# A Strassen scheme for the up projection of four batches, and a joint read in the down projection

## The chip, the cores and the metric

The kernel runs on one core of a Trainium2 chip. A core has five engines that run side by side, each through its own list of instructions in order, held together by semaphores: TensorE (PE in the profile; matrix products, results in PSUM), VectorE (DVE), ScalarE (ACT), GpSimd (POOL; here only DMA issue) and SyncE (SP; DMA issue). PSUM has eight banks of 128 x 512 fp32; SBUF is the working memory.

The metric is the device time of one execution in microseconds (us). The kernel before takes 298.88 us, the median of 3 runs (298.83 to 299.14). The profiled execution spans 296.9 us from its first to its last instruction; profile times count from that start.

## What is computed

The program is a block-causal attention followed by an MLP mixer, for 8 batches, 576 positions, 8 heads of 64 (so 512 model columns). The reference, cut to what matters:

```python
# attention: q, k, v are (8, 8, 576, 64); blocks of 64 positions
scores = scale * q @ k.T                       # per batch and head
scores = where(block_i >= block_j, scores, -1e9)
attn = exp(scores - max) / (sum + 1e-9)
x = (attn @ v)                                 # as (8, 576, 512)

# mixer
h  = relu(x.T @ w_tok1) @ w_tok2               # over positions: 576 -> 256 -> 576
u  = x + h.T
h2 = relu(u @ w_ch1) @ w_ch2                   # over channels: 512 -> 1536 -> 512
out = u + h2                                   # float32
```

`u @ w_ch1` is called the up projection, `(...) @ w_ch2` the down projection. Matrix inputs are bf16, sums fp32.

## The kernel before

The kernel is written as a list of operations with dependencies, estimated costs and priorities. On the host a list scheduler (`Plan`) places them on the engines, tries 1000 random changes of the priorities, and issues the best order that it found. So a change of any operation can change the order of all.

Of each batch, 512 positions are treated on their own, and the last 64 of two batches together ("mixed" rows). The PSUM banks are split: four hold scores, as two pairs (`sc`), four are the general pool `mm`.

```python
sc = ring(2, [128, 2, 512], FP32, "sc", psum)     # 4 banks: scores
mm = ring(4, [128, 512], FP32, "mm", psum)        # 4 banks: all else
gT = ring(2, [128, NDC, 512], BF16, "gT")         # relu(u @ w_ch1), NDC = 12 blocks of 128 channels
sums = ring(3, [128, 3, NDC // 2, 128], BF16, "sums")
```

The up projection: for each of 12 blocks of hidden channels, four matmuls of 512 columns add up in a bank (L950), and ACT or DVE clips it at zero into `gT` (L725, L727).

```python
def channel_up(b, uT_done, wc1_ready, prio):
    for cc in range(NDC):
        def emit(o, ...):
            for m in range(NDM):                     # NDM = 4
                nc.tensor.matmul(out=bank_of(bank), lhsT=wc1_sb[:, m, channels(cc)],
                                 rhs=uT[b % 2][:, :, m, :], start=(m == 0), stop=(m == NDM - 1))   # L950
        op = P.add("PE", ..., take=[(BANK, bank)])
        def emit(o, ...):
            relu(o, gT[b % 2][:, cc, :], bank_of(bank))                        # L725 ACT, L727 DVE
        done.append(P.add(EVAC, evac_cost(512), emit, [op], prio, give=[bank]))
```

The down projection of batches 1 to 7 is already a Strassen scheme (the Winograd form): the product is cut into 2 x 2 blocks, and seven block products stand in for eight. The input sums are made on DVE from `gT` (L1032), products gather in banks (L1049), and DVE adds what a bank holds into the output tile after each product, so the bank goes on gathering (L1071). Rows 128 t and 128 t + 256 are one pair; t = 0, 1 are done one after the other.

```python
def channel_down_fast(b, g_done, wc2_ready, u_done, prio):
    for t in range(2):
        r1, r2 = slice(128 * t, 128 * t + 128), slice(128 * t + 256, 128 * t + 384)
        a11, a12 = gt[:, 0:H6, r1], gt[:, H6:NDC, r1]                      # H6 = 6
        a21, a22 = gt[:, 0:H6, r2], gt[:, H6:NDC, r2]
        for key, dst, x, y, op in (("s1", s1, a21, a22, ADD), ("s2", s2, s1, a11, SUB),
                                   ("s4", s4, a12, s2, SUB), ("s3", a21, a11, a21, SUB)):
            nc.vector.tensor_tensor(out=dst, in0=x, in1=y, op=op)          # L1032, 768 elements
        # product: six matmuls of 256 columns into one bank                  L1049
        # fold: o_sb[...] = bank[:, 0:256] + (u or o_sb)                     L1071
        fold("a", 0, 0, product(0, "a", a11, b11, []), True, False)
        fold("e", 1, 1, product(1, "e", s1, w1_, [made["s1"]]), True, False)
        ...                                                                # seven in all
```

Around it: token mixing makes `u` (matmuls L739 and L832, the addition of x on DVE at L847), a DMA transposes it into `uT` (a ring of two), and attention has scores (L511), exponentials on ACT (L530), the product with v (L558) and its scaling on DVE (L586). `L396` turns q and k from staging memory on DVE, `L1009` makes the sums of the down weights, `L356` copies a bank or a staged input.

Of the kernel before, what the change touches and what calls it, by code (L numbers as in the profile page):

```python
# [195 lines left out]
def kernel(  # L196
# [11 lines left out]
    nc = tc.nc  # L208
# [18 lines left out]
    qraw = ring(3, [128, NB, D], BF16, "qraw")  # L227
    kraw = ring(3, [128, NB, D], BF16, "kraw")

    qT = ring(3, [128, S, 2], BF16, "qT")  # L230
    kT = ring(3, [128, 640, 2], BF16, "kT")
    v1 = ring(2, [128, 5, H, 66], BF16, "v1")
    e_sb = ring(2, [128, 4, 1600], BF16, "e_sb")
    et_sb = ring(2, [128, 640], BF16, "et_sb")
# [8 lines left out]
    sums = ring(3, [128, 3, NDC // 2, 128], BF16, "sums")  # L243
    o_sb = ring(3, [128, 2, DM], FP32, "o_sb")
# [22 lines left out]
    BANK = ("mm",)  # L267
    WARM, KEEP = 16, 110

    def bank_of(note):  # L270
        return mm[note["slot"]]
# [256 lines left out]
    def exp(dst, n, op, note, prio, urgent=0):  # L528
        def emit(o):
            nc.scalar.activation(dst, sc[SC.index(note["pool"])][:, :, 0:n], EXP, scale=scale)  # L530

        return P.add("ACT", act_cost(2 * n), emit, [op], prio, give=[note], urgent=urgent)

    def mask(e, c, hs, deps, prio, urgent=0):
        def emit(o):
            nc.vector.memset(e[64:128, hs, c : c + 64], 0.0)  # L536

        return P.add("DVE", 0.1, emit, deps, prio, urgent=urgent)

    def head_out(b, head, deps, prio, tail, urgent=0):  # L540
# [41 lines left out]
        rc = P.add("DVE", 0.12, emit_rc, [av] + reuse(("rinv", head % 4)), prio - 1, urgent=urgent)  # L582
# [93 lines left out]
    def attention(b, ready, v_ready):  # L676
# [5 lines left out]
        def exps_of(op, notes, dst, n, prio):  # L682
            return [exp(dst[:, 2 * f : 2 * f + 2], n, op, notes[f], prio) for f in range(2)]
# [11 lines left out]
        tail_done = None  # L695
        for hg in range(2):
            e = e_sb[hg]
            prio = base + 4 * hg
            e_war = reuse(("e", hg))
            exps = [[], []]  # L700
            for s, regions in enumerate(SETS):
                n = sum(w for _, _, _, w in regions)
                parts = tuple((hg,) + r for r in regions)
                notes = [{}, {}]
                pools = [(SC[f : f + 1], notes[f]) for f in range(2)]
                op = score_set(b, parts, range(4), ready[hg] + e_war, prio + 0.1 * s, pools)
                these = exps_of(op, notes, e[:, :, 512 * s : 512 * s + n], n, prio + 0.1 * s)
                masks = [mask(e, c, slice(0, 4), these, prio) for c in MASKS[s]]
                for f in range(2):
                    exps[f] += [these[f]] + masks  # L710
            if tail_done is None:
                tail_done = tail()
            for h in range(4):
                deps = exps[h // 2] + v_ready[hg] + x_war + pad + pads["e", hg]
                done.append(head_out(b, 4 * hg + h, deps, prio + 1, tail_done[h // 2]))
# [89 lines left out]
    def token_mix(b, x_done, w1_ready, w2_ready):  # L805
        odd = b % 2
        pair = b // 2
        xt, at, ut, umt = x_sb[b % 3], aT[b % 2], u_sb[b % 3], um_sb[pair % 2]
        prio = -990.5 + 10 * b
        a_war = reuse(("a", b % 2))  # L810
        u_war = reuse(("u", b % 3))
# [77 lines left out]
        for f in range(2 if crossbar else 0):  # L889
# [7 lines left out]
            reads(("u", b % 3), op)  # L897
# [8 lines left out]
        for si in () if crossbar or b == 0 else range(4 + odd):  # L906
# [15 lines left out]
            reads(("u", b % 3) if si < 4 else ("um", pair % 2), op)  # L922
# [74 lines left out]

    H6 = NDC // 2
# [14 lines left out]
    def channel_down_fast(b, g_done, wc2_ready, u_done, prio):  # L1013
        gt, ut = gT[b % 2], u_sb[b % 3]
        for t in range(2):
            oi = out_n[0] % 3
            out_n[0] += 1
            o_war = reuse(("o", oi))
            si = sum_n[0] % 3
            sum_n[0] += 1  # L1020
            s_war = reuse(("s", si))
            r1, r2 = slice(128 * t, 128 * t + 128), slice(128 * t + 256, 128 * t + 384)
            a11, a12 = gt[:, 0:H6, r1], gt[:, H6:NDC, r1]
            a21, a22 = gt[:, 0:H6, r2], gt[:, H6:NDC, r2]
            s1, s2, s4 = (sums[si][:, n] for n in range(3))
            made = {}
            prev = None
            for key, dst, x, y, op in (
                ("s1", s1, a21, a22, ADD), ("s2", s2, s1, a11, SUB), ("s4", s4, a12, s2, SUB), ("s3", a21, a11, a21, SUB),
            ):  # L1030
                def emit(o, dst=dst, x=x, y=y, op=op):
                    nc.vector.tensor_tensor(out=dst, in0=x, in1=y, op=op)  # L1032

                prev = made[key] = P.add(
                    "DVE", dve_cost(768, 2), emit, (g_done + s_war if prev is None else [prev]), prio - 2 + 0.1 * t
                )
                reads(("g", b % 2), prev)
            b11, b21, b22 = wc2_sb[:, 0:H6, 0:256], wc2_sb[:, H6:NDC, 0:256], wc2_sb[:, H6:NDC, 256:512]
            w1_, w2_, w3_, w4_ = (wd_sb[:, n] for n in range(4))
            banks = {"a": {}, "c": {}, "e": {}}  # L1040
            last = {}
            stored = []

            def product(n, to, x, y, deps):
                bank, first = banks[to], to not in last

                def emit(o):
                    for kk in range(H6):
                        nc.tensor.matmul(  # L1049
                            out=bank_of(bank)[:, 0:256], lhsT=x[:, kk], rhs=y[:, kk],  # L1050
                            start=first and kk == 0, stop=kk == H6 - 1,
                            skip_group_check=not first,
                        )

                op = P.add(
                    "PE", mm_cost(256, H6), emit, deps + g_done + wc2_ready + wd_ready + [last.get(to)],
                    prio + 0.2 * t + 0.02 * n, take=[(BANK, bank)] if first else (),
                )
                reads(("g", b % 2), op)
                reads(("s", si), op)  # L1060
                last[to] = op
                return op

            def fold(to, row, col, op, residual, final):
                dst = o_sb[oi][:, row, 256 * col : 256 * col + 256]
                bank = banks[to]

                other = ut[:, t + 2 * row, 256 * col : 256 * col + 256] if residual else dst

                def emit(o):  # L1070
                    nc.vector.tensor_tensor(out=dst, in0=bank_of(bank)[:, 0:256], in1=other, op=ADD)  # L1071

                done = P.add(
                    "DVE", dve_cost(256), emit, [op, folded.get((row, col))] + u_done + o_war, prio - 1,
                    give=[bank] if final else (),
                )
                reads(("u", b % 3), done)
                folded[row, col] = last[to] = done
                return done

            folded = {}
            fold("a", 0, 0, product(0, "a", a11, b11, []), True, False)
            fold("e", 1, 1, product(1, "e", s1, w1_, [made["s1"]]), True, False)
            fold("a", 0, 1, product(2, "a", s2, w2_, [made["s2"]]), True, False)
            fold("e", 0, 1, product(3, "e", s4, b22, [made["s4"]]), False, True)
            fold("a", 1, 1, product(4, "a", a21, w3_, [made["s3"]]), False, False)
            fold("c", 0, 0, product(5, "c", a12, b21, []), False, True)
            fold("a", 1, 0, product(6, "a", a22, w4_, []), True, True)

            rows = out[b, 0:512, :].rearrange("(c t p) d -> t p c d", c=2, t=2)[t]  # L1090
            if b == B - 1 and t == 1:
                pieces = [(0, 0, 2), (1, 1, 2), (1, 0, 1)]
            else:
                pieces = [(None, 0, 2)]
            for row, c0, c1 in pieces:
                def emit(o, row=row, c0=c0, c1=c1, oi=oi, rows=rows):
                    cols = slice(256 * c0, 256 * c1)
                    if row is None:
                        nc.sync.dma_start(out=rows, in_=o_sb[oi])
                    else:  # L1100
                        nc.sync.dma_start(out=rows[:, row, cols], in_=o_sb[oi][:, row, cols])

                deps = [folded[r, c] for r in ((0, 1) if row is None else (row,)) for c in range(c0, c1)]
                size = (2 if row is None else 1) * (c1 - c0) / 2
                reads(("o", oi), P.add("SP", 0.5, emit, deps, prio, xfer=8 * 0.086 * size))
# [4 lines left out]
    def channel_down(b, g_done, wc2_ready, u_done, prio, mixed=False):  # L1110
        chunks = [None] if mixed else list(range(4))
        gt = gmT[0] if mixed else gT[b % 2]
        ut = um_sb[b // 2 % 2] if mixed else u_sb[b % 3]
# [3 lines left out]
        for n, si in enumerate(chunks):  # L1117
# [4 lines left out]
            if n % 2 == 0:  # L1122
                oi = out_n[0] % 3
# [3 lines left out]
            for cols in (slice(0, 256), slice(256, 512)) if last else (slice(0, 512),):  # L1127
# [32 lines left out]
                reads(("gm", 0) if mixed else ("g", b % 2), prev)  # L1160
# [15 lines left out]
                reads(("um", b // 2 % 2) if mixed else ("u", b % 3), op)  # L1176
# [36 lines left out]
    x_done = {}  # L1213
    for b in range(B + 1):
# [8 lines left out]
        if b > 0:  # L1223
            p = b - 1
            uT_done, um_done, u_done, um_rows = token_mix(p, x_done[p], w1_ready, w2_ready)
            g_done = channel_up(p, uT_done, wc1_ready, 10 * p + 2)
            if p == 0:
                channel_down(p, g_done, wc2_ready, u_done, 10 * p + 4)
            elif p < B - 1:
                channel_down_fast(p, g_done, wc2_ready, u_done, 10 * p + 4)  # L1230
            if p % 2 == 1:
                gm_done = channel_up_mixed(p // 2, um_done, wc1_ready, 10 * p + 3.5)
                prio = 10 * p + (5 if p < B - 1 else 3.9)
# [37 lines left out]
```

The softmax here doesn't subtract the row's maximum and nothing guards it: scores larger than these inputs give would overflow.

## Time and profile before

| | value |
|---|---|
| time, median of 3 | 298.88 us |
| span of the profiled execution | 296.9 us |
| TensorE matmuls busy | 290.8 us, 3257 instructions |
| VectorE busy | 203.7 us, 509 instructions |
| ScalarE busy | 164.4 us, 233 instructions |
| granted TensorE clock | 1.000 of full speed |
| up projection (L950) | 384 matmuls of 512 columns |
| clips of the up projection into `gT` | 76 on ACT, mean 597 ns; 20 on DVE, mean 688 ns |

The page gives for each engine its busy time, then the span in 40 equal slices in which a digit is the busy share in tenths, then the chain of work that ended last, by engine and by line, and then groups of instructions (line, engine, operation, out<-in, shape, number, busy us, mean ns). A table by stretches of time gives, for each stretch, its length and each engine's busy us with the number of instructions. Matmuls overlap one another in the pipeline, so the mean of one is longer than the time that it adds to a row of them.

### The profile page before, as it was taken

What the parts mean: (1) busy time and instruction counts of PE and PEld (TensorE: products, weight loads), DVE (VectorE), ACT (ScalarE), POOL (GpSimd) and SP (SyncE); (2) the same over time, 40 slices, a digit from 0 to 9 for tenths busy, and PEclk for the clock granted to TensorE, in tenths of its full rate; (3) what the DMA queues carried; (4) which work ended last, traced back from release to release, by engine and by line L of the source; (5) the groups of instructions that cost most, each with busy time, mean ns of one, the idle gap of its engine ahead of it and who ended that gap; (6) DMA issues with size and microseconds to landing.
All of it is one profiled execution on the core that took longest, in us unless ns stands there. A gap on an engine that the chain in (4) does not pass through costs nothing.

```text
span 296.9 us, 7686 instructions
## 1 busy us (share of the span) xinstructions
PE 290.8 (98%) x3257; PEld 184.7 (62%) x3276; DVE 203.7 (69%) x509; ACT 164.4 (55%) x233; POOL 62.0 (21%) x96
## 2 busy tenths in 40 slices
PE   8999999999999999999999999999999999999995
PEld 3576456465557855546764567774586677558774
DVE  5566879899679979959988787665086085028284
ACT  5896755578767566686666664624612611670400
POOL 9776363701700070340040000000000000000000
PEclk9999999999999999999999999999999999999999
DMA  9999999992992299991239022211033043100314
GB/s 210 183 196 202 212 182 189 222 215 66 163 133 41 42 137 203 198 131 35 41 56 168 2 20 53 91 47 62 2 71 144 0 91 109 68 2 0 145 31 148
DMA packets 64387, 31.99 MB, mean 108 GB/s; under 512 B 53088, under 2 KB 55008, under 8 KB 64352
## 3 DMA queue, kind: packets, MB, share of 16 engines
q0 software_dynamic: 44320, 17.34, 49.0%
q1 hardware_dynamic: 19744, 13.57, 17.4%
q8 instruction: 25, 0.41, 0.5%
q10 hardware_dynamic: 288, 0.59, 0.5%
q14 instruction: 10, 0.08, 0.1%
HBM read 35.85 MB, written 9.44 MB: 153 GB/s over the span
## 4 chain that ended last, share of the span: by engine, by line
PE 95%; DMA 2%; DVE 1%; ACT 1%; issue 1%; ACTq 0%
PE mm L950 28%; PE mm L1049 22%; PE mm L558 10%; PE sc L511 10%; PE mm L1144 7%; PE mm L739 6%; PE mm L832 4%; PE mm L977 4%; DMA gT<-in_q_dram 2%; PE mm L863 1%; ACT e_sb L530 1%; PE mm L783 1%; PE mm L335 0%; PE mm L913 0%; DVE u_sb L847 0%
## 5 line engine op out<-in xcount | busy, mean ns | idle before, releaser
L530 ACT ACTIVATE e_sb<-sc 128x1024 bf16<-128x1024 f32 x95 | 92.6, 1028 | 30.8 <-PE sc L511 30.5
L950 PE MATMUL mm<-uT,wc_sb 128*128 128x512 bf16 x384 | 89.6, 380 | 0.0
L725 ACT ACTIVATE gT<-mm 128x512 bf16<-128x512 f32 x76 | 45.4, 597 | 64.8 <-PE mm L950 53.9
L950 PEld LDWEIGHTS <-wc_sb 128*128 128x128 bf16 x384 | 41.7, 114 | 37.1 <-issue 3.6
L425 POOL DMA_DIRECT2D v<-in_v_dram x45 | 37.1, 837 | 33.5 <-PE mm L1049 22.4
L1049 PEld LDWEIGHTS <-gT 128*128 128x128 bf16 x336 | 32.0, 98 | 6.7 <-issue 1.7
L511 PE MATMUL sc<-qT,kT 32*128 32x64 bf16 (+4 forms) x744 | 35.4, 281 | 0.4 <-DVE qT L396 0.3
L558 PEld LDWEIGHTS <-e_sb 128*128 128x128 bf16 x896 | 31.5, 97 | 6.6 <-issue 3.1
L558 PE MATMUL mm<-v,e_sb 128*128 128x65 bf16 x896 | 34.3, 193 | 0.0
L586 DVE TENSOR_TENSOR x_sb<-mm,rinv 128x320 bf16<-128x320 f32 x64 | 31.2, 491 | 2.2
L1032 DVE TENSOR_TENSOR sums<-gT 128x768 bf16<-128x768 bf16 x14 | 7.2, 555 | 36.4 <-ACT gT L725 36.4
L1071 DVE TENSOR_TENSOR o_sb<-mm,u_sb 128x256 f32<-128x256 f32 x56 | 23.1, 420 | 7.7 <-PE mm L1049 6.8
L1049 PEld LDWEIGHTS <-sums 128*128 128x128 bf16 x252 | 24.3, 98 | 5.6 <-DVE e_sb L536 0.4
L847 DVE TENSOR_TENSOR u_sb<-mm,x_sb 128x512 bf16<-128x512 f32 x28 | 17.8, 685 | 7.9 <-PE mm L832 6.6
L511 PEld LDWEIGHTS <-kT 32*128 32x128 bf16 x752 | 12.4, 93 | 17.1 <-issue 13.8
L1071 DVE TENSOR_TENSOR o_sb<-mm,o_sb 128x256 f32<-128x256 f32 x42 | 17.4, 421 | 7.5 <-PE mm L1049 7.1
L396 DVE STREAM_TRANSPOSE kT<-kraw 128x288 int32<-128x288 int32 x32 | 21.0, 705 | 1.8 <-ACT kraw L356 1.6
L1049 PE MATMUL mm<-wc_sb,gT 128*128 128x256 bf16 x168 | 22.0, 273 | 0.0
L1049 PE MATMUL mm<-wd_sb,gT 128*128 128x256 bf16 x168 | 21.9, 273 | 0.0
L1049 PE MATMUL mm<-wd_sb,sums 128*128 128x256 bf16 x168 | 21.4, 273 | 0.0
L396 DVE STREAM_TRANSPOSE qT<-qraw 128x288 int32<-128x288 int32 x32 | 21.0, 705 | 0.6 <-PE sc L511 0.3
L727 DVE TENSOR_SCALAR gT<-mm 128x512 bf16<-128x512 f32 x20 | 13.8, 688 | 7.6 <-PE mm L950 7.2
(78 smaller groups left out, 285.2 us busy)
## 6 DMA issues: line engine op xcount, KB each, us to landing
out_dram<-o_sb SPq DMA_DIRECT2D x15, 512.0 KB, 3.2
qraw<-in_q_dram POOLq DMA_DIRECT2D x15, 288.0 KB, 7.1
kraw<-in_k_dram POOLq DMA_DIRECT2D x15, 288.0 KB, 6.8
v<-in_v_dram POOLq DMA_DIRECT2D x28, 128.0 KB, 6.7
wc_sb<-in_moe_w_ch_dram POOLq DMA_DIRECT2D x8, 192.0 KB, 7.2
wc_sb<-in_moe_w_ch_dram POOLq DMA_DIRECT2D x3, 512.0 KB, 10.8
out_dram<-o_sb SPq DMA_DIRECT2D x10, 128.0 KB, 2.4
v<-in_v_dram POOLq DMA_DIRECT2D x15, 64.0 KB, 5.9
```

The source lines that it names most:

```text
L396: nc.vector.transpose(dst[:, 0:S, :] .rearrange("p s e -> p (s e)") .bitcast(I32) .rearrange("p (a k) -> p k a", k=NB)[:, k0:k1], raw2.bit ...
L425: nc.gpsimd.dma_start(out=dst, in_=src)
L511: nc.tensor.matmul(out=home(n)[:, c0 : c0 + w], lhsT=kT[i][r, j0 : j0 + 128, par], rhs=qT[i][r, i0 : i0 + w, par], start=(par == 0), stop= ...
L530: nc.scalar.activation(dst, sc[SC.index(note["pool"])][:, :, 0:n], EXP, scale=scale)
L558: nc.tensor.matmul(out=u[:, I, 0:65], lhsT=w, rhs=vt[:, J, head, 0:65], start=(J == 0), stop=(J == I),)
L586: nc.vector.tensor_tensor(out=xt[:, :, 64 * head : 64 * head + 64], in0=u[:, :, 0:64], in1=ri.to_broadcast([128, 5, 64]), op=MULT,)
L725: nc.scalar.activation(dst, src, RELU)
L739: nc.tensor.matmul(out=bank_of(bank)[:, w * n : w * n + w], lhsT=wt[:, tt : tt + 255 : 2], rhs=xt[:, c, cols], start=(c == 0), stop=(c == 4),)
L950: nc.tensor.matmul(out=bank_of(bank), lhsT=wc1_sb[:, m, channels(cc)], rhs=uT[b % 2][:, :, m, :], start=(m == 0), stop=(m == NDM - 1),)
L1049: nc.tensor.matmul(out=bank_of(bank)[:, 0:256], lhsT=x[:, kk], rhs=y[:, kk], start=first and kk == 0, stop=kk == H6 - 1, skip_group_check= ...
L1071: nc.vector.tensor_tensor(out=dst, in0=bank_of(bank)[:, 0:256], in1=other, op=ADD)
L1144: nc.tensor.matmul(out=ps, lhsT=gt[:, cc, c0 : c0 + 128], rhs=wc2_sb[:, cc, cols], start=(cc == 0 and not turned), stop=(cc == NDC - 1),)
```

## The change

The up projection of batches 4 to 7 becomes a Strassen scheme too. Two batches (4 and 5, then 6 and 7) make one product: the 2 x 2 cut is two blocks of hidden channels by the two batches in the result, and two halves of the 512 model columns inside. Seven products of two 512-column matmuls take the place of eight. The sums of weights are made once, those of the inputs once for each pair, on DVE. As the results share partial sums, what a bank holds is copied to an fp32 tile by ACT or DVE ("keep"), the bank goes on gathering, and a later bank is added to such a copy on DVE ("join"). Joined results are clipped at zero afterwards in SBUF ("clip"); one result in four is clipped straight from its bank.

To find memory, tiles are put together and used twice: weight sums lie over the q/k staging tiles, input sums and `u` of batch 7 over the first tile of exponentials, the kept parts over the second, and `gT` of batches 6 and 7 over the turned q/k and over v. After the last scores the four score banks join the general pool as "late".

The down projection of batches 1 to 6 reads both row pairs at once: a sum covers 1536 elements instead of 768, a product is twelve matmuls into a full bank, and a fold covers 512 columns. Batch 7 keeps the two steps. Some cost estimates and priorities are changed with it. The diff, cut to its core:

```diff
-    sums = ring(3, [128, 3, NDC // 2, 128], BF16, "sums")
-    o_sb = ring(3, [128, 2, DM], FP32, "o_sb")
+    sums = ring(5, [128, NDC // 2, 256], BF16, "sums")
+    o_sb = ring(4, [128, 2, DM], FP32, "o_sb")
...
+    ws_sb = raws...[:, 0 : 4 * DC]            # weight sums, over the q/k staging
+    ts_sb = e_flat[0][:, 0:4096]...           # input sums, over the first tile of exponentials
+    u_last = e_flat[0][:, 4096:6144]...
+    g_last = [... for t in (turned..., vals)]
+    part = [e_flat[1].bitcast(FP32)[:, 1536 * i : 1536 * (i + 1)]... for i in range(2)]
...
-    BANK = ("mm",)
+    P.pool("late", [])                        # filled by the last exponentials
+    BANK = ("mm", "late")
+    FAST_UP = 4
...
+    def up_weight_sums(wc1_ready):
+        for dst, x, y, op in ((w[0], a21, a22, ADD), (w[1], w[0], a11, SUB), (w[2], a11, a21, SUB), (w[3], a12, w[1], SUB)):
+            nc.vector.tensor_tensor(out=dst, in0=x, in1=y, op=op)
+
+    def channel_up_fast(b, uT_done, wc1_ready, prio):
+        g_war = g_free(b - 1) + g_free(b)
+        e_ended.extend(reuse(("e", 0)) + reuse(("e", 1)))
+        e_war = e_ended + reuse(("ts", 0))
+        b11, b12, b21, b22 = (uT[n][:, :, j : j + 2, :] for j in (0, 2) for n in range(2))
+        for n, dst, x, y in ((0, t[0], b12, b11), (1, t[1], b22, t[0]), (2, t[2], b22, b12), (3, t[3], b21, t[1])):
+            nc.vector.tensor_tensor(out=dst, in0=x, in1=y, op=SUB)
+        for n in range(NDC // 2):
+            ...
+            # product: two matmuls of 512 columns; keep: cast(bank -> part), ACT or DVE
+            # join: g = bank + part, DVE; clip: g = max(g, 0), ACT or DVE
+            r1 = keep(0, "a", product(0, "a", a_of(0, 0), b11, base))
+            r6 = keep(1, "e", product(1, "e", s_of(0), t[0], [made[0]] + ws_ready))
+            r2 = keep(2, "a", product(3, "a", s_of(1), t[1], [made[1]] + ws_ready))
+            r5 = join(0, c1, 0, "c", [product(2, "c", a_of(0, 1), b21, base), r1], True)
+            clip(0, slice(c1, c1 + 1), [r5])
+            r7 = join(1, c1, 2, "e", [product(4, "e", s_of(3), b22, base + ws_ready), r2], True)
+            r3 = join(1, c2, 1, "a", [product(5, "a", s_of(2), t[2], [made[2]] + ws_ready), r6], False)
+            clip(1, slice(c1, c2 + 1, 2), [r7, r3])
+            op = product(6, "a", a_of(1, 1), t[3], [made[3]] + wc1)
+            ...                                  # relu from bank "a" into g[0][:, c2]
...
     def channel_down_fast(b, g_done, wc2_ready, u_done, prio):
-        for t in range(2):
+        joint = b < B - 1
+        for ts in ((0, 1),) if joint else ((0,), (1,)):
+            c0, nt = ts[0], len(ts)
...
-                    "DVE", dve_cost(768, 2), emit, ...
+                    "DVE", dve_cost(768 * nt, 2), emit, ...
...
+                    for i in range(nt):
+                        for kk in range(H6):
+                            nc.tensor.matmul(
+                                out=bank_of(bank)[:, 256 * i : 256 * i + 256],
+                                lhsT=x[:, kk, 128 * i : 128 * i + 128], rhs=y[:, kk], ...)
...
+    def fast_pair():
+        p = held[1][0]
+        pair = channel_up_fast(p, held[0][1] + held[1][1], wc1_ready, 10 * p - 8 if p < B - 1 else 44.1)
+        for n in range(2):
+            if held[n][0] < B - 1:
+                channel_down_fast(held[n][0], pair[n], wc2_ready, held[n][2], 10 * p - 6 + n)
```

Smaller numbers in the last arguments are higher priorities: the pair of 4 and 5 has 42, down 4 has 44 and down 5 has 45, the pair of 6 and 7 has 44.1, down 6 has 64 and down 7 has 74.

## The prediction

> **What bounds the kernel now.** I read the page from the top: busy times, then the 40 slices, then the chain that ended last, and after that two tables by stretches of time.
>
> ```profile
> PE 290.8 (98%) x3257; PEld 184.7 (62%) x3276; DVE 203.7 (69%) x509; ACT 164.4 (55%) x233; POOL 62.0 (21%) x96
> ...
> PE   8999999999999999999999999999999999999995
> ...
> DVE  5566879899679979959988787665086085028284
> ACT  5896755578767566686666664624612611670400
> ...
> PE 95%; DMA 2%; DVE 1%; ACT 1%; issue 1%; ACTq 0%
> PE mm L950 28%; PE mm L1049 22%; PE mm L558 10%; PE sc L511 10%; PE mm L1144 7%; PE mm L739 6%; PE mm L832 4%; PE mm L977 4%; DMA gT<-in_q_dram 2%; PE mm L863 1%; ACT e_sb L530 1%; PE mm L783 1%; PE mm L335 0%; PE mm L913 0%; DVE u_sb L847 0%
> ```
>
> The matmul row is 9 in every slice but the first and the last, and 95% of the last-ending chain is TensorE. A busy PE is not by itself a PE at its peak, so I ask whether the matmuls stand end to end. The chain has a piece of 72 up-projection matmuls (L950) that takes 15.54 us: 15.54 / 72 = **0.216 us each**. The mean of 380 ns in the groups is overlapped time and not a cost. So only fewer matmuls, or fewer columns, can shorten the body of this kernel, and each up-projection matmul removed is worth 0.216 us if nothing else stops PE.
>
> Next, in which stage does the change lie? Scores (L511) are the mark of attention; the first two rows below are of that line alone, the others of everything.
>
> ```profile
> 180.00:200.00 20.00, 2.42 (x60) 0.80 (x56) 1.00 0.21 55
> 200.00:220.00 20.00, 0.00 (x0) 0.00 (x0) 1.00 0.21 53
> ```
>
> ```profile
> core 0: us, PE busy (x) PEld busy (x) DVE busy (x) ACT busy (x) POOL busy (x), PEclk, DMA share, GB/s
> 199.00:293.60 94.60, 94.29 (x672) 64.53 (x674) 45.10 (x101) 33.43 (x56) 0.00 (x0) 1.00 0.21 63
> ...
> 140.00:160.00 20.00, 19.89 (x244) 13.10 (x244) 18.18 (x46) 12.76 (x15) 4.19 (x5) 1.00 0.66 82
> ```
>
> Attention is over near 199 us. From there to 293.6 us, which I call **the tail**, PE is busy 94.29 of 94.60 us, DVE only 45.10, ACT 33.43. The groups of L950 alone show 190 of its 384 matmuls in the tail, which is four batches of 48 but for two. So batches 4 to 7, the ones that the change touches, already do their channel mixing in the tail. The last row shows that 18.18 of 20 us on DVE did not keep PE from 19.89: a crowded DVE is not by itself a stopped PE.
>
> **What the Trainium skill says.** "TensorE: Matmul & The Clock Gate", section "Wait — 56ns, not 53.3ns?", puts back-to-back matmuls of 512 columns at 215.7 ns; the trace agrees (0.216), so the matmuls have nothing left to give but their number. "VectorE: DVE Perf Modes", section "The perf-mode tier table (the rule you actually need)": tensor_tensor runs at twice the base rate for 16-bit data in SBUF and at the base rate with a PSUM operand, and a tensor_scalar on 16-bit SBUF data at four times. The trace agrees with the first two: 1,536 bf16 elements take 953 ns (L1009), 768 take 550 (L1032); from PSUM 256 take 420 (L1071) and 512 take 685 (L847), so (685 - 420) / 256 = 1.035 ns an element and about 155 ns fixed. No run here shows the third yet. "ScalarE: Activation LUTs", section "What ACT_TABLE_LOAD costs": back-to-back ACTIVATEs overlap by about 93 ns; here two exponentials of 1,028 ns take 1.94 us together, about 0.11 less than their sum. "PSUM — Partial Sum Buffer", section "PSUM bank collisions raise a hardware error": engines mustn't touch one bank at once. So in a bank that gathers several products, every product must wait for the reader of the one before; the new scheme lives by such banks.
>
> **The change, part by part.** Take a unit as one pair of batches and two blocks of hidden channels.
>
> *Removed from PE.* Before, a unit is 2 batches x 2 blocks x 4 = 16 matmuls; after, 7 products x 2 = 14. Two pairs x 6 units x 2 = 24 matmuls fewer, 24 x 0.216 = **5.2 us less**. A unit takes 14 x 0.216 = 3.0 us of PE. The down projection has the same number and width of matmuls as before: 0 on PE.
>
> *Added on the evacuating engines, per unit.* Before: four clips from PSUM to gT, 597 ns each on ACT. After: three copies and one clip, which can all lie on ACT (597; a PSUM copy to fp32 is 586 at L356), so ACT keeps its 2.4 us; three joins with a PSUM operand, DVE only, 3 x 0.685 = 2.06 us; and two clips inside SBUF of 512 and 1,024 elements, on DVE by the skill's four-fold rate an estimate of 0.155 + 512 x 0.26 ns = 0.29 and 0.155 + 1024 x 0.26 ns = 0.42 us. Over 12 units: 24.7 us of joins and 8.5 us of clips. The planner may put clips on ACT.
>
> *Input sums.* Four per pair over 1,024 bf16: between 550 ns at 768 and 953 at 1,536, so about 0.68; 8 x 0.68 = 5.5 us. Weight sums: four over 1,536 elements in steps of two, between 0.95 us (double rate) and 0.155 + 1.59 = 1.75 us (base rate): 4 to 7 us, once. They need the q/k staging memory, and L396, its last reader, runs for the last time near 170 us; DVE has about 3 us in each 14 free from 171 to 199, so I expect these mostly before the tail.
>
> *Down projection, both chunk pairs at once.* Per batch before: 8 sums x 0.55 + 14 folds x 0.42 = 10.3 us of DVE. After: 4 x 0.95 + 7 x 0.685 = 8.6. For batches 4, 5 and 6 in the tail this gives back 3 x 1.7 = 5 us; batches 1 to 3 win as much in the attention stage, where PE stands at 168.17 of 169 us (30 to 199 us) and so cannot turn it into time.
>
> *Sum for the tail.* PE 94.3 - 5.2 = 89.1 us. DVE 45.1 + 24.7 + 8.5 + 5.5 - 5.1 = 78.7 us, or up to 85 if all weight sums fall there. DVE goes from 48% to 88 to 95% of the tail. PE stays the bound by the sums, but with little room. ACT stays near 33, so moving clips there can bring DVE to about 70.
>
> *What is moved.* The sums and kept parts of the new scheme lie in the memory of the exponentials, so no unit of batches 4 and 5 can begin before the last attention product. As attention ends when batches 0 to 3 are just done, this holds little back. Then the transposed inputs of 6 and 7 can land only when all units of 4 and 5 are read; PE has down 4 and down 5 (84 matmuls, 9.17 us each in the chain) and the mixed rows of 4 and 5 to fill that. Units of 6 and 7 rank ahead of down 5, so it can fill their gaps too. After attention the score banks are lent out, so there are 8 instead of 4 banks.
>
> **The rivals.**
>
> *DVE becomes the bound.* In the first 20 to 28 us after 199, DVE has six units (6 x 2.77 = 16.6 us with clips), four input sums (2.7), four u additions (2.5 in the trace), two mixed additions (1.4), the last attention scalings and perhaps weight sums: 24 to 31 us, against PE 18 us of units plus about 10 us of token mixing and mixed rows. For: the sums are close. Against: the row at 140 us, and ACT at a third. If it happens PE idles 3 to 7 us: 297 to 301 us.
>
> *The chain inside a bank becomes the wait.* The main bank of a unit goes product, copy, product, copy, product, join, product, clip: 4 x 0.43 + 3 x 0.6 + 0.685 = 4.2 us and some 0.2 us for each of 7 hand-overs (DVE starts about 0.23 us after it went idle behind PE near 290 us), so 5.6 us for 3.0 us of PE. Two units must be in flight, with up to three banks each: six banks. With eight it fits, with four it would not: 2.6 us lost x 6 units = 16 us for a pair. For: if the score banks come late. Against: they are free when the units begin. If half a pair suffers: 302 us or more.
>
> *The gain is kept whole.* Nothing new waits: 298.9 - 5.2 = 293.7. More than this needs PE time that the change doesn't touch; in the tail there is 0.3 us of idle PE, in 30 to 199 us 0.8 us, so below 293 only a better start (the first 20 us have 1.6 us idle) helps.
>
> **Range and chances.** I expect 5.2 us off and about 1.2 us of it given back in the hand-overs at 199 us, between the pairs, and from the last unit to down 6: 298.9 - 5.2 + 1.2 = **294.9 us**. The low end, 292.6, is the whole gain and one us from a luckier order elsewhere, since every order is planned anew; the high end, 298.6, is a DVE stall that eats almost all. Faster by over 2% means below 292.9, more than the matmuls hold: 0.09. Slower by over 2% means above 304.9, some 11 us of new idle PE: 0.06. Within 2%: 0.85.
>
> **What would show it.** The page after should have 24 fewer 512-column matmuls between the up groups, and PE busy about 5 us lower. In the tail PE should stay above 97% and DVE stand at 75 to 90%; a PE idle of several us behind a join or an input sum would show the first rival, behind a copy or clip on ACT the second. Joins should be near 685 ns, clips in SBUF near 0.3 and 0.4 us on DVE, weight sums at 0.95 to 1.75 us and before 199 us. I am wrong if attention ends later than about 200 us, if clips in SBUF run at the base rate, or if the planned order misjudges DVE.

## The result, and the profile after

The changed kernel takes **296.88 us** (median of 4 runs, 296.54 to 297.26) against 298.86 us before: ratio 0.9935, 95% interval 0.9917 to 0.9953. It is 2.0 us faster. The prediction had 4.0 us, so its size was wrong by half, although the time lies inside the range.

The page of the kernel after, the lines that answer to those of before:

```profile
PE 285.8 (97%) x3232; PEld 180.4 (61%) x3252; DVE 236.4 (80%) x512; ACT 166.9 (57%) x236; POOL 62.1 (21%) x96
...
PE   8999999999999999999999999999999999989994
...
DVE  5566668988859979959988978678998968959993
ACT  5897874667776564786566685524476004847000
...
PE 87%; ACT 6%; DVE 4%; DMA 1%; issue 1%; ACTq 0%; DVEq 0%
```

PE is busy 5.0 us less, as it should be with 24 matmuls fewer. But the matmul row now has an 8 late in the kernel, and the chain that ended last is no longer 95% PE: 10% of it are pieces of ACT and DVE. The tail by the table of stretches:

```profile
199.00:293.60 94.60, 90.13 (x650) 60.39 (x650) 79.43 (x134) 35.44 (x58) 0.00 (x0) 1.00 0.23 66
```

PE 90.13 (predicted 89.1), DVE 79.43 (predicted 78.7), ACT 35.44 (predicted near 33): the work is what the prediction summed up. Yet the last matmul ends at 291.0 us instead of 293.5, which is 2.5 us earlier and not 5.2. The view of who waited for whom, of PE in the kernel after, names what PE stood still for:

```profile
PE sc L1097 <- DVE o_sb L1244: 0.9, 1, 0.9
PE sc L1097 <- ACT e_sb L393: 0.5, 2, 0.3
...
PE sc L874 <- DVE gT L1125: 0.3, 1, 0.3
```

Each row gives the waiter, the one waited for, us in total, times, and the longest. The kernel before has no such wait in its tail. The columns show pure idle time; measured from one start to the next, the four matmuls come 664, 665, 572 and 1,327 ns after the one ahead of them instead of 216, near 206, 209, 220 and 262 us, so together they cost 0.45 + 0.45 + 0.36 + 1.11 = **2.4 us**. One thing is common to all four: the waiting matmul writes a bank named `sc`, that is, a score bank lent out as "late".

The timeline of the longest one, in the kernel after (start, us, engine, line, operation, in brackets the idle time and its releaser):

```profile
259.62 0.59 PE L1097 MATMUL sc<-e_sb,raws 128*128 128x512 bf16 x2
...
260.06 1.47 PE L1221 MATMUL sc<-wd_sb,gT 128*128 128x256 bf16 x12
...
261.57 0.69 DVE L395 COPY e_sb<-sc 128x512 f32<-128x512 f32 x1 [1.05 <-PE sc L1221]
...
262.18 0.68 DVE L1244 TENSOR_TENSOR o_sb<-sc,u_sb 128x512 f32<-128x512 f32 x1
...
262.91 0.59 PE L1097 MATMUL sc<-uT,raws 128*128 128x512 bf16 x2 [0.95 <-DVE o_sb L1244]
```

The copy at 261.57 is the "keep" of the product at 259.62. That product is done near 260.2, but the copy waits 1.05 us for L1221, a product of the *down* projection that it doesn't use. Then the next product of the unit, whose bank the copy left free, waits for the fold L1244, which reads that other product. The list of instructions tells why: the copy and the two L1097 matmuls use the first half of the tile `sc0`, L1221 and L1244 use its second half. These are two PSUM banks, but one tile, and the waits that the framework puts in were ordered by the tile. Following each wait of the program to the instruction that it names, I find 18 waits in the kernel after that join an instruction on one half of a score tile with one on the other half whose data it doesn't use; in the kernel before there is none.

So the **theory**: the missing 2.4 us are waits between the halves of one tile. The rivals are those of the prediction: the first, that DVE at 79 of 92 us is in truth the bound, and the second, that the chain of product and reader in one bank is. A third is that the order found by the random search was unlucky.

### The profile page after: what moved, and what is told of

Read it like the earlier page. It is cut to its first block, busy times and chain, and to the rows that moved or that the text cites. A ratio compares the mean times of both kernels' runs of the same rounds, so it can differ in the third digit from the quotient of the medians.

```text
span 294.8 us, 7653 instructions
## 1 busy us (share of the span) xinstructions
PE 285.8 (97%) x3232; PEld 180.4 (61%) x3252; DVE 236.4 (80%) x512; ACT 166.9 (57%) x236; POOL 62.1 (21%) x96
## 4 chain that ended last, share of the span: by engine, by line
PE 87%; ACT 6%; DVE 4%; DMA 1%; issue 1%; ACTq 0%; DVEq 0%
PE mm L1221 17%; PE mm L992 15%; PE sc L548 9%; PE mm L595 9%; PE mm L1312 7%; PE mm L781 6%; PE sc L1097 5%; PE mm L1097 5%; PE sc L1221 4%; ACT e_sb L567 4%; PE mm L874 4%; PE mm L1019 3%; DVE turned L433 2%; DMA gT<-in_k_dram 1%; DVE gT L1125 1%
## 5 line engine op out<-in xcount | busy, mean ns | idle before, releaser
L992 PE MATMUL mm<-uT,wc_sb 128*128 128x512 bf16 x192 | 46.1, 382 | 0.0
L462 POOL DMA_DIRECT2D vals<-in_v_dram x45 | 37.0, 837 | 27.0 <-PE mm L595 22.4
L433 DVE STREAM_TRANSPOSE turned<-raws 128x288 int32<-128x288 int32 x64 | 40.2, 707 | 2.4 <-ACT raws L393 1.5
L548 PE MATMUL sc<-turned 32*128 32x64 bf16 (+4 forms) x744 | 35.4, 281 | 1.0 <-ACT e_sb L567 0.4
L992 PEld LDWEIGHTS <-wc_sb 128*128 128x128 bf16 x192 | 20.0, 115 | 20.7 <-issue 5.7
L595 PE MATMUL mm<-vals,e_sb 128*128 128x65 bf16 x868 | 32.5, 193 | 0.1
L1221 PEld LDWEIGHTS <-sums 128*128 128x128 bf16 x252 | 24.1, 98 | 4.5 <-issue 1.2
L1221 PEld LDWEIGHTS <-gT 128*128 128x128 bf16 x240 | 22.9, 98 | 4.5 <-issue 1.3
L548 PEld LDWEIGHTS <-turned 32*128 32x128 bf16 x752 | 12.8, 93 | 19.3 <-issue 16.7
L767 ACT ACTIVATE gT<-mm 128x512 bf16<-128x512 f32 x24 | 14.3, 597 | 10.9 <-PE mm L992 10.8
L781 PE MATMUL mm<-x_sb,w_sb 128*128 128x512 bf16 (+1 forms) x97 | 17.6, 313 | 0.3
L1244 DVE TENSOR_TENSOR o_sb<-mm,u_sb 128x512 f32<-128x512 f32 x20 | 13.7, 687 | 3.4 <-PE mm L1221 2.6
L1097 PEld LDWEIGHTS <-raws 128*128 128x128 bf16 x96 | 9.2, 98 | 10.9 <-issue 1.5
L1221 PE MATMUL mm<-wd_sb,sums 128*128 128x256 bf16 x132 | 15.7, 273 | 0.0
```

Of the source, the lines that this page charges most:

```text
L433: nc.vector.transpose(dst[:, 0:S, :] .rearrange("p s e -> p (s e)") .bitcast(I32) .rearrange("p (a k) -> p k a", k=NB)[:, k0:k1], raw2.bit ...
L462: nc.gpsimd.dma_start(out=dst, in_=src)
L548: nc.tensor.matmul(out=home(n)[:, c0 : c0 + w], lhsT=kT[i][r, j0 : j0 + 128, par], rhs=qT[i][r, i0 : i0 + w, par], start=(par == 0), stop= ...
L595: nc.tensor.matmul(out=u[:, I, 0:65], lhsT=w, rhs=vt[:, J, head, 0:65], start=(J == 0), stop=(J == I),)
L781: nc.tensor.matmul(out=bank_of(bank)[:, w * n : w * n + w], lhsT=wt[:, tt : tt + 255 : 2], rhs=xt[:, c, cols], start=(c == 0), stop=(c == 4),)
L1097: nc.tensor.matmul(out=bank_of(bank), lhsT=x(m), rhs=y[:, :, m, :], start=first and m == 0, stop=m == 1, skip_group_check=not first,)
```

## The experiments

All ratios are to the kernel before, run on the same chip.

**Own banks.** The score tiles lie in a memory pool of their own, which is closed at the first use of a late bank; the same memory is then given out as four tiles of one bank. The planned order stays the same, instruction for instruction.

```diff
-    sc = ring(2, [128, 2, 512], FP32, "sc", psum)
+    sc_pool = tc.tile_pool(name="scores", bufs=1, space=bass.MemoryType.PSUM)
+    sc = ring(2, [128, 2, 512], FP32, "sc", sc_pool.__enter__())
+    late = []
+    def late_bank(n):
+        if not late:
+            sc_pool.__exit__(None, None, None)
+            late_pool = ctx.enter_context(tc.tile_pool(name="late", ...PSUM))
+            late.extend(ring(4, [128, 512], FP32, "late", late_pool))
+        return late[n]
...
-        return mm[n] if note["pool"] == "mm" else sc[n // 2][:, n % 2]
+        return mm[n] if note["pool"] == "mm" else late_bank(n)
```

> The changed kernel, with the four late banks as four tiles of their own instead of halves of the two score tiles; the planned order is the same to the last instruction. Theory (waits between two halves of one tile): the four PE stalls of 0.45, 0.45, 0.35 and 1.1 us near 206, 209, 220 and 262 us go, 296.9 - 2.3 = 294.6 us, PE ends near 288.7 us. Rival 1 (DVE load is the bound of the tail): DVE has the same work in the same order, the stalls stay, 296.9 us. Rival 2 (chain of product and reader inside one bank): the chain is the same, 296.9 us.

Measured: **294.1 us, ratio 0.9855 (0.9836 to 0.9873)**. The interval lies wholly below that of the change, 0.9917 to 0.9953; the difference of the ratios, 0.0080 x 298.9, is 2.4 us. The time is 0.5 us below the expected one. Set side by side, the two traces have the same list of matmuls, and until 205 us their starts differ by less than 0.1 us. The kernel with own banks then gains in steps: 0.45, 0.45, 0.36 and 1.11 us at the four matmuls, and 0.15 and 0.12 us at two others (219.16 and 222.22 us), **2.6 us** at the end. Here is the same place in the timeline of the kernel with own banks, some 1.5 us earlier by then:

```profile
258.11 0.59 PE L1107 MATMUL late<-e_sb,raws 128*128 128x512 bf16 x2
...
258.54 1.47 PE L1231 MATMUL late<-wd_sb,gT 128*128 128x256 bf16 x12
...
259.11 0.69 DVE L405 COPY e_sb<-late 128x512 f32<-128x512 f32 x1
...
260.28 0.59 PE L1107 MATMUL late<-uT,raws 128*128 128x512 bf16 x2
```

The copy now starts while the other product is still running, and no row of the up projection is left among the waits of PE. The table of stretches in the kernel with own banks:

```profile
199.00:293.60 94.60, 89.22 (x650) 60.43 (x650) 79.09 (x134) 35.24 (x58) 0.00 (x0) 0.99 0.24 66
```

The end of the chain that ended last (start, us, what), in the kernel before, after, and with own banks:

```profile
293.54 0.42 DVE o_sb L1071
```

```profile
291.04 0.42 DVE o_sb L1244
```

```profile
287.72 0.67 PE mm L1231 x6
288.39 0.02 issue
288.41 0.42 DVE o_sb L1254
```

DVE does the same 79 us of work in the tail, and the last fold starts at 288.41 us instead of 293.54 before: 5.1 us, all but 0.1 of the worth of 24 matmuls. The same DVE work and the same chains with another time: rivals 1 and 2 don't explain the missing time.

**Another order, with and without halves.** Only the seed of the planner's search is changed, first in the changed kernel, then in the one with own banks.

```diff
-        rnd = random.Random(0)
+        rnd = random.Random(1)
```

> The changed kernel as it is, with halves of tiles, and another seed of the planner's random search: another order with the planner's own end 0.4 us later. Theory (waits between halves cost in any order that uses late banks): 296 to 298 us, with PE stalls on score banks in the tail again, at other times. Rival (the order on record was an unlucky one): 294.5 to 295 us.

> The order of the run before with seed 1, instruction for instruction, but with the four late banks as tiles of their own. Theory: all of what that order lost in the tail was waits between halves, so it falls from 298.9 to 294.5 us (0.4 above own banks with the first order, as the planner has it). Rival (the order of seed 1 is bad by itself): it stays near 298 us.

Measured: 298.92 us with halves, ratio 1.0002 (0.9992 to 1.0012), so **nothing at all is gained**; 295.44 us with own banks, ratio 0.9864 (0.9848 to 0.9881). The expectation for the first, 296 to 298, was too low, and that for the second was 0.9 us too low. The last matmul ends where it was expected, at 288.7 us against 288.4 in the first order with own banks. What was not foreseen lies behind it: from the start of the last fold to the end of the span there are 5.2 us instead of 3.8. The changed kernel with this order has 27 waits between halves instead of 18, and the waits of PE show a part of them:

```profile
PE sc L1097 <- ACT e_sb L393: 1.0, 1, 1.0
PE sc L1097 <- DVE gT L1125: 0.5, 1, 0.5
PE sc L1097 <- DVE vals L1125: 0.2, 1, 0.2
PE sc L1097 <- DVE e_sb L889: 0.2, 1, 0.2
```

With own banks none of these four is left. They are pure idle time, 1.9 us in all. Set side by side matmul by matmul, the kernel with own banks is about 0.2 us ahead when the tail begins and 3.95 us at the end; the six largest steps, of 0.24 to 1.18 us, all lie at matmuls into score banks. So the loss isn't that of one unlucky order. What luck decides is how much the halves cost: 2.4 us in one order, (1.0002 - 0.9864) x 299 = 4.1 us in another.

**A third order with own banks** (seed 2).

> Own banks with a third order, whose end the planner puts 0.2 us before that of own banks with the first. Theory: without waits between halves the chip follows the plan, so 293.5 to 294.5 us; orders now differ by half a us and no more. If it is over 295.5, the order matters by itself, and a part of what the halves were charged with is luck.

Measured: ratio 0.9842 (0.9819 to 0.9865), median 294.26 us, as expected; a fourth run, 300.68 us at a granted clock of 0.97, is left out as slow. With three orders the ratios with own banks are 0.9855, 0.9864 and 0.9842, so the orders differ by up to 0.0022 x 299 = 0.7 us where I expected half a us; the intervals overlap.

**Six late and general banks instead of eight.** The changed kernel, but only one half of each score tile is lent out.

```diff
-            freed = [[{"pool": "late", "slot": 2 * f + i} for i in range(2)] if last else None ...]
+            freed = [[{"pool": "late", "slot": 2 * f}] if last else None ...]
```

> The changed kernel with only one bank of each score tile lent out, so six general banks in the tail, none sharing a tile with another in use. Theory: no wait between halves is left, and the planner's own estimate of its end is the same with six as with eight, so about 294.6 us in spite of two banks fewer. Rival 1: 296.9 us. Rival 2: fewer banks mean fewer units in flight, so slower than the changed kernel, 298 us or more.

Measured: 295.86 us, ratio 0.9906 (0.9890 to 0.9921). This lies between the 294.6 us of the theory and the 296.9 of rival 1, and its interval overlaps that of the change, so the time alone decides little. The profile shows a loss at the other end of the kernel. The stretch from 10 to 20 us, in the kernel with six banks and in the kernel after:

```profile
10.00:20.00 10.00, 9.13 (x121) 5.77 (x120) 3.64 (x18) 8.22 (x16) 8.10 (x15) 0.66 1.48 187
```

```profile
10.00:20.00 10.00, 9.68 (x159) 5.91 (x158) 5.49 (x25) 10.00 (x20) 8.53 (x15) 1.00 1.48 189
```

The third column from the right is the granted clock: 0.66 against 1.00 (own banks have 1.00 too). The new order put in 18 filler matmuls (L372) in the first 17 us, the other two 30. That the fewer fillers are the reason was not tested. In the tail no row of the up projection is left among its waits of PE. From its last matmul of attention to its last matmul of all it takes 91.2 us, against 93.0 in the change and 90.4 with own banks; as the order is another, this is a rough comparison. It agrees with the theory.

**Four banks.** No late banks.

```diff
-    BANK = ("mm", "late")
+    BANK = ("mm",)
```

> The changed kernel with no late banks at all: four general banks to the end. No wait between halves can be there. Theory and rival 1: the planner sees 4.5 us lost to the lack of banks, so about 294.6 + 4.5 = 299 us. Rival 2 in the strong form of the prediction (16 us lost for a pair): 310 us or more. The size tells how much the chain inside a bank is worth when the banks are short.

Measured: 297.44 us, ratio 0.9959 (0.9944 to 0.9974): 0.0104 x 298.8 = 3.1 us slower than own banks, not the 16 us for a pair that the prediction reckoned with, nor the 4.5 of the planner. And it is within about 0.7 us of the change, with intervals that overlap: **in this order, four banks lent out as halves of two tiles were worth little more than no banks lent out**.

**More work on DVE.** Own banks, with one of the three joins of each unit done twice, or three times, into the same place.

```diff
-                    nc.vector.tensor_tensor(out=dst, in0=bank_of(bank), in1=src, op=ADD)
+                    for _ in range(times):          # times = 2 or 3 for the first join
+                        nc.vector.tensor_tensor(out=dst, in0=bank_of(bank), in1=src, op=ADD)
```

> Own banks, and one join of each unit is done twice over with the same result: 12 more DVE operations of about 0.6 us, 7.2 us more DVE work in the tail, 86 of 89 us. Theory (PE is the bound and the order is good): up to 1 us later, 294.1 to 295.1. Rival (DVE load is what costs): most of the 7.2 us, 298 us or more.

> As before, but that join three times: 14.4 us more DVE work, 93 us in a tail whose PE work is 89. DVE must now be the bound by the sums: 3 to 5 us later than own banks, 297 to 299 us. If it is not later, the sums of DVE work say nothing on this stage.

The joins took longer than I had reckoned: by the traces the 12 added ones are 8.1 us of work and the 24 are 16.4, not 7.2 and 14.4. Measured: 293.98 us, ratio 0.9837 (0.9821 to 0.9853), with 8.1 us more DVE work: no cost that can be seen. With 16.4 us more, 296.26 us, ratio 0.9915 (0.9898 to 0.9931): 0.0060 x 299 = 1.8 us slower than own banks. I expected 3 to 5. The tables of stretches of the two, in this order, say more:

```profile
199.00:293.60 94.60, 90.19 (x704) 61.68 (x705) 83.33 (x142) 39.54 (x66) 0.00 (x0) 1.00 0.25 66
```

```profile
199.00:293.60 94.60, 90.38 (x648) 60.04 (x647) 86.69 (x144) 39.41 (x67) 0.00 (x0) 1.00 0.23 66
```

In the tail DVE rises by 4.2 and 7.6 us only, and ACT by 4.3 and 4.2: the planner moved work that either engine can do over to ACT, and in the second kernel some DVE work to before 199 us (159.8 us there instead of 157.0). So neither run put its whole added work on DVE in the tail, and neither is the clean overload that I had planned. In the second, PE does wait for joins (L1137), 0.6 us at most in one row, and also in the general banks (0.5 us). So DVE can hold PE up, but 83 us of work in the 90 of the tail did not, and the change has 79. Rival 1 falls.

**One part alone.** The up projection alone, with own banks, and the down projection alone, with all else as before.

```diff
-        joint = b < B - 1          # up alone: every batch in two steps
+        joint = False
...
-    FAST_UP = 4                    # down alone: no pair goes through the Strassen scheme
+    FAST_UP = 8
```

> Own banks, but the down projection of batches 1 to 6 in two steps as before the change: 10.3 instead of 8.6 us of DVE per batch, the same matmuls on PE. Theory (PE is the bound of the tail once the waits between halves are gone, DVE has room): 294.1 to 294.8 us, so the joint down projection is worth half a us at most. Rival (DVE is near its limit, at 79 of 89 us): 5 us more on DVE in the tail show as 2 us or more, 296 us.

> Only the joint down projection of batches 1 to 6; the up projection, its banks and its memory as before. PE has the same matmuls, so all theories expect the time of before, 298.9 us within 0.5; if the joint down projection by itself costs time at the front or the end of the kernel it is 299.5 or more, and that would be part of the missing gain.

Measured: up alone 294.6 us, ratio 0.9853 (0.9837 to 0.9870), the same as own banks with both parts; down alone 299.1 us, ratio 1.0015 (0.9993 to 1.0037), the same as before. DVE in the tail of the first is at 81.6 us, only 2.5 above own banks and not 5, as that order also changed. The joint down projection saves DVE work, and is worth nothing that these runs can measure.

## Why the prediction was wrong, point by point

- **PE bounds the tail, and a matmul removed is worth 0.216 us.** Right. PE is 5.0 us less busy, and with own banks the last fold starts 5.1 us earlier.
- **The work on DVE and ACT.** Right, in the sum and in its terms. Joins take 681 to 693 ns (predicted 685), clips on DVE 289 and 424 ns (290 and 420). The Trainium skill's "VectorE: DVE Perf Modes", section "The perf-mode tier table (the rule you actually need)", gives a tensor_scalar on bf16 data in SBUF four times the base rate, and the trace agrees: (424 - 289) / 512 = 0.26 ns an element, a quarter of the 1.035 from PSUM. Input sums take about 0.68 us. The weight sums take 0.95 us, the lower of the two figures, and lie at 169 to 179 us, ahead of the tail.
- **The hand-overs give back 1.2 us.** This is the step that failed. 2.5 us earlier at the end of PE, with 5.2 us of matmuls gone, are 2.7 us given back there; the trace shows 2.4 of it in four waits, and own banks bring the last fold forward by 2.6. Three of the four waits don't lie at the places that I named, 199 us, between the pairs, and from the last unit to down 6, but inside the units, and one at 206 us in the token mixing (L874). With own banks all hand-overs together cost next to nothing: 5.2 - 5.1 = 0.1 us.
- **"After attention the score banks are lent out, so there are 8 instead of 4 banks."** This sentence holds the error. I counted banks and did not ask by what unit a wait is ordered. The changed kernel shows it: `sc[n // 2][:, n % 2]` is a slice of a tile that two banks share. The Trainium skill's "PSUM — Partial Sum Buffer", section "PSUM bank collisions raise a hardware error", asks that accesses of two engines to one bank be kept apart by semaphores; I took from it that other banks are free. With own banks that held (the copy at 259.11 us runs beside a product in another bank), but with halves the program waited by tile. A rival "the lent banks are tied together in pairs" was missing.
- **The chain inside a bank.** As a danger with four banks it was named rightly and sized wrongly: 3.1 us and not 16 for a pair. Why it is so much less was not traced; the order was planned anew for four banks.
- **DVE as a bound.** Right to reject it: with 8.1 us of added joins the time doesn't change, and a loss (1.8 us) appears only with 16.4 us.

What is still between 294.1 and the 293.7 of "the gain is kept whole" lies behind the matmuls. From the start of the last fold to the end of the span there were 296.9 - 293.54 = 3.4 us before and 292.2 - 288.41 = 3.8 us with own banks. The cause stays open. This stretch changes with the order: it is 3.2 us (292.7 - 289.42) with the first join done twice and 5.2 us with seed 1, although batch 7 writes its output in the same pieces in all three.

## What to carry to other kernels

Before counting buffers as gained, ask what the ordering is tied to: if two buffers are slices of one tile, an instruction on one may wait for work on the other, and here that ate half of the gain. The sign in a profile is an idle time whose releaser touches the same tile name but not the data; the cure here was to give the memory out again as separate tiles. And when a part of the time is missing, set the traces of two kernels with the same order side by side: the places where one gains on the other are the places of the loss.

## What was not expected of the hardware

In the kernel with six banks, the granted clock averaged 0.66 between 10 and 20 us, with 18 filler matmuls at the start, and 1.00 in the changed kernel, with 30. Whether the fillers are the reason was not tested. Weight sums over bf16 elements in pairs, with gaps between the pairs, took 0.95 us for 1,536 elements, as long as without gaps (0.95 at L1009 in the kernel before).
